# A transformer block on one core: GpSimd makes the attention factors by a power of -1, and ScalarE does some of its work at other places of a step

## The chip, the cores and the metric

The kernel runs on one core of one Trainium2 chip. The metric is the time of one execution on the device in microseconds. Before the change the median of three runs is 760.0 us (758.47 to 761.76). All times below are microseconds unless marked ns.

A core has five engines that run side by side, each in the order of its own program: TensorE (PE; its weight loads are PEld), VectorE (DVE), ScalarE (ACT), GpSimd (POOL) and SyncE (SP, which here only issues DMAs). They wait for each other by semaphores. GpSimd and ScalarE issue DMAs too.

## The reference

One block of an adaptive transformer, with x of 2048 rows and D = 640, in fp32:

```python
sa, ca, ga, sb, cb, gb = split(silu(c) @ w_mod, 6)
h = layernorm(x) * (1 + ca) + sa
x = x + ga * attention(h)
h = layernorm(x) * (1 + cb) + sb
x = x + gb * ((relu(h @ w1 + b1) ** 2) @ w2 + b2)          # F = 1728
```

Attention has 32 heads of 20 and is linear in the number of rows:

```python
q, k, v = split(h @ wqkv)                     # per head
pq, pk = q @ w_phi, k @ w_phi
phi_q = concat(softmax(pq), softmax(-pq))     # 40 features per head
phi_k = concat(softmax(pk), softmax(-pk))
kv, z = phi_k.T @ v, sum over rows of phi_k
o = (phi_q @ kv) / (phi_q @ z + 1e-6)
attention = o @ wo
```

## The kernel before

Matrix products run in fp32r with both operands split into a high and a low part: the high part is a rounding copy on ScalarE, the low part a subtraction on VectorE, and each product is made of three (high by high, high by low, low by high). So every tensor that TensorE reads goes through both engines first.

The rows are 16 tiles of 128, `t` = 0 to 15; two tiles make a step `j` = 0 to 7. The program has three parts. The first projects q, k and v of all tiles and sums `kv` and `z`. For 12 tiles the exponentials of q (`e`: two halves, of pq and of -pq, not yet normalized) go to DRAM and come back later as `el`; those of the last four tiles (`eq12` to `eq15`) stay on the chip, and the last three of them are still raw products when the second part starts. The second part, which the change edits, is the attention output. The third is the MLP of all steps.

In the second part, for each tile:

- `e_prod` (L875): VectorE multiplies `el` with a row of z (`scr`, L879) and sums within heads (`dn`, L881). GpSimd makes the common denominator `dd` of both softmaxes from these sums and the sums `rs_q` of the exponentials: two instructions for the 1e-6 term (L884, L885), then per half one product (L887) and one addition (L888).
- `e_recip` (L890): VectorE takes the reciprocal of `dd` (L894) and multiplies it with the other half's `rs_q` to the two factors `dn` (L896).
- `e_scale`: VectorE scales `e` by the factors: the last two heads to `ut` (`e_tail`, L906), the other thirty to `ezb` (`e_main`, L917). Here these scaled exponentials are called e'.

Then for each step: TensorE turns `ut` (`tail_turn`, L933), ScalarE copies the result to `ept` (L934), and TensorE multiplies that with a small part of kv (`tail_num`, L939), which ScalarE puts into the last four columns of `ezb` (L942). TensorE turns `ezb` in five groups (`te`, L951), ScalarE copies each (`ept`, L952), TensorE multiplies them with kv to `numa`, `numb`, `numc` (`num`), ScalarE copies the high half of the attention output `ot` (L974), and VectorE makes the low half (`num_lo`, L89; in steps 0 and 1 it goes another way, by TensorE and ScalarE). Last comes the product with `wo` (`do_wo`, `pwo`), which ScalarE copies to `at` (L1011) and stores.

All engines but SP follow the order in which the code of this part is written (`manual_schedule`). The loop over `j` interleaves two steps: `do_wo` of step j is cut into pieces, and at fixed places between them (`turns`) stand the tail and the `te` of step j + 1. Between those the loop places other work: `q_chain` and `exps` of the raw tiles 13 to 15 (VectorE's maximum, minimum and subtraction, ScalarE's two exponentials; `SPREAD` and `SUMS` say in which step), `p_hi` (ScalarE's high half of a weight of the MLP, L1043), `ln0` (the pieces of the first LayerNorm of the MLP: two sums, two squares, copies of the statistics, four scalings, four scalings), and `plus_x` (DMAs on GpSimd's queue that add x to the stored rows).

Of the kernel before, what the change touches and what calls it, by code (L numbers as in the profile page):

```python
# [8 lines left out]
F32 = mybir.dt.float32  # L9
# [3 lines left out]
ALU = mybir.AluOpType  # L13
AX = mybir.AxisListType

P = 128
S = 2048
D = 640
H = 32
DH = 20  # L20
F = 1728
NT = S // P
# [13 lines left out]
KEPT = NT - POSTPONED  # L36
W2_AT = 48
PLAIN = 2
DEALT = range(NT // 2)
DIRECT = 2  # L40
LAST = 3
W_AT = (
    *range(21),
# [9 lines left out]
def kernel(  # L53
# [19 lines left out]
    nc = tc.nc  # L73
# [23 lines left out]
    const = ctx.enter_context(tc.tile_pool(name="const", bufs=1))  # L97
# [10 lines left out]
    def tok2(tag, name, at=0, pool=None):  # L108

        bufs = 1  # L110
        if tag == "w":
            tag = f"w{next(w_at)}"
        elif pool is None:
            bufs = BUFS.get(tag, 1)
        t = (pool or mem).tile([P, 2 * D + (W2_AT if tag == 'late' else 128 if tag in W_LONG else 0)], F32, tag=tag, name=name, bufs=bufs)
        return t[:, at : at + 2 * D].rearrange("p (s d) -> p s d", s=2)
# [16 lines left out]
    def small(shape, tag, name, bufs=2):  # L133
        return (pc if tag in ("mx", "sk", "dn", "dd") else tiny).tile(shape, F32, tag=tag, name=name, bufs=bufs)
# [94 lines left out]
    def flat(e):  # L229
        return e.rearrange("p s d -> p (s d)")  # L230
# [27 lines left out]

    cs = const.tile([P, NC], F32, name="cs")
    ce = const.tile([P, NC], F32, name="ce")  # L260
    const.tile([P, 8], F32, name="fill")
    nc.scalar.activation(ce, c_t, AF.Exp, scale=-1.0)
    nc.vector.tensor_scalar(ce, ce, 1.0, None, op0=ALU.add)
    nc.vector.reciprocal(ce, ce)
# [114 lines left out]
    HT, PK, EK, EQ, PQ = {}, {}, {}, {}, {}  # L379
# [54 lines left out]
    def spread(t, e, nm):  # L434
        mx = small([P, 2, H], "mx", f"mx{nm}")
        nc.vector.tensor_reduce(mx[:, 0], heads(t), axis=AX.X, op=ALU.max)
        nc.vector.tensor_reduce(mx[:, 1], heads(t), axis=AX.X, op=ALU.min)
        for s in (1, 0):
            nc.vector.tensor_tensor(heads(e[:, s]), heads(t), over(mx[:, s]), op=ALU.subtract)

    def exps(e):
        nc.scalar.activation(e[:, 0], e[:, 0], AF.Exp)  # L442
        nc.scalar.activation(e[:, 1], e[:, 1], AF.Exp, scale=-1.0)
# [28 lines left out]
    def q_chain(t, whole=True):  # L472
        if t < KEPT:
            EQ[t] = tok2(f"q{t % 2}", f"eq{t}")
        e = EQ[t]
        spread(PQ[t], e, f"q{t}")
        if whole:
            exps(e)
            q_sums(t)

    def q_sums(t):
        e = EQ[t]
        s = rs_q[:, t]
        nc.vector.tensor_reduce(s, heads(flat(e)), axis=AX.X, op=ALU.add)
        if t < KEPT:
            nc.sync.dma_start(ESP[t], flat(e))
# [225 lines left out]
    for t in range(2, NT - 2):  # L712
        j, i = divmod(t, 2)
# [161 lines left out]
    def e_prod(t):  # L875
        if t >= NT:
            return
        z = SCR[t % 2]
        nc.vector.tensor_tensor(z, flat(ET[t]), flat(zb), op=ALU.mult)  # L879
        dn = DN[t] = small([P, 2, H], "dn", f"dn{t}", 3)  # L880
        nc.vector.tensor_reduce(dn.rearrange("p s h -> p (s h)"), heads(z), axis=AX.X, op=ALU.add)  # L881
        rs = rs_q[:, t].rearrange("p (s h) -> p s h", s=2)
        dd = DD[t] = small([P, H], "dd", f"dd{t}")
        nc.gpsimd.tensor_tensor(dd, rs[:, 0], rs[:, 1], op=ALU.mult)  # L884
        nc.gpsimd.tensor_scalar(dd, dd, 1e-6, None, op0=ALU.mult)  # L885
        for s in range(2):
            nc.gpsimd.tensor_tensor(dn[:, s], dn[:, s], rs[:, 1 - s], op=ALU.mult)  # L887
            nc.gpsimd.tensor_tensor(dd, dd, dn[:, s], op=ALU.add)  # L888

    def e_recip(t):  # L890
        if t >= NT:
            return
        rs = rs_q[:, t].rearrange("p (s h) -> p s h", s=2)
        nc.vector.reciprocal(DD[t], DD[t])  # L894
        for s in range(2):
            nc.vector.tensor_tensor(DN[t][:, s], rs[:, 1 - s], DD[t], op=ALU.mult)  # L896
# [26 lines left out]
    def e_scale(t):  # L923
        e_tail(t)
        e_main(t)
# [46 lines left out]
    def num_hi(j):  # L972
        for src, hi, _ in num_parts(j):
            nc.scalar.activation(hi, src, AF.Copy)  # L974

    def num_lo(j):

        if j >= DIRECT:
            for src, hi, low in num_parts(j):
# [9 lines left out]
    def do_wo(j, i, h, *hooks, a=0, b=15):  # L989
        for at, hook in hooks:  # L990
            if at > a:
                wo_part(j, i, h, a, at)
            hook()
            a = at
        if a < b:
            wo_part(j, i, h, a, b)
# [73 lines left out]
    def p_hi(n=1):  # L1070
        for _ in range(n):
            if todo["hi"]:
                prep_hi(*todo["hi"].pop(0))
# [139 lines left out]
    SPREAD, SUMS = {1: 1, 3: 2}, {3: 1, 4: 2}  # L1213
    ln0 = None
    for j in range(NB):
        nxt = j + 1 < NB
        b, c = 2 * j + 5, 2 * j + 6
        turns = {1: ((0, 0, 11), (0, 0, 15), (0, 1, 4), (0, 1, 15)), 6: ((0, 1, 2), (0, 1, 8), (0, 1, 15), (1, 0, 15)),
                 0: ((0, 1, 4), (0, 1, 10), (1, 0, 3), (1, 0, 15))}.get(j, ((0, 0, 6), (0, 0, 11), (0, 0, 15), (0, 1, 15)))
        todo_ = (lambda: tail_turn(j + 1), lambda: tail_num(j + 1), lambda: tr_e(j + 1, range(3)), lambda: tr_e(j + 1, (3, 4)))  # L1220

        def hooks(i, h):
            return [(at, f) for (i_, h_, at), f in zip(turns, todo_) if nxt and (i, h) == (i_, h_)]
        if j == 4:
            load_x1(0)
            load_dealt(0)
        if j < 5:
            p_load()
        if j != 5:
            e_prod(b)  # L1230
        e_recip(b - 1)
        e_scale(b - 1)
        if j == 6:
            mod_sum(5, gate_b)
        if j == 5:
            q_chain(KEPT + 3, False)
        load_e(b + 2)
        do_wo(j, 0, 0, *hooks(0, 0))
        if j == 5:
            exps(EQ[KEPT + 3])  # L1240
            q_sums(KEPT + 3)
            e_prod(b)
        do_wo(j, 0, 1, *hooks(0, 1))
        if j == 7:
            t2(0, 0)
            t2(0, 1)
        if j == 4:
            ln0 = ln_dealt(0)
            next(ln0)
            next(ln0)  # L1250
        if j == 6:
            next(ln0)
            turn(0, 0)
            turn(0, 1)
        if j == 2:
            exps(EQ[KEPT + 1])
        if j in SUMS:
            q_sums(KEPT + SUMS[j])
        e_prod(c)
        if j != 5:  # L1260
            e_recip(b)
            e_scale(b)
        do_wo(j, 1, 0, *hooks(1, 0))
        if j == 7:
            t2(0, 2)
            t2(0, 3)
        if nxt:
            num(j + 1)
            num_hi(j + 1)
        do_wo(j, 1, 1, b=8)  # L1270
        if j == 7:
            t2(0, 4)
            p = tp("gbt")[:NC, :P]
            nc.tensor.transpose(p, gate_b, ident)
            nc.scalar.activation(gate_r, p, AF.Copy)
            nc.sync.dma_start(GD[1], gate_r)
            nc.sync.dma_start(gb_b, GD[1].rearrange("c p -> (c p)")[None, :].to_broadcast([P, D]))
        if not nxt:
            do_wo(j, 1, 1, a=8)
        if nxt:  # L1280
            do_wo(j, 1, 1, a=8, b=11)
            num_lo(j + 1)
            do_wo(j, 1, 1, a=11)
        if j == 5:
            e_recip(b)
            e_scale(b)
        if 1 <= j < 6:
            p_hi()
        if j in SPREAD:
            q_chain(KEPT + SPREAD[j], False)  # L1290
            if j > 1:
                exps(EQ[KEPT + SPREAD[j]])
        load_e(c + 2)
        if j:
            plus_x(j - 1)
        if j == 4:
            next(ln0)
            next(ln0)
            next(ln0)
        if j == 5:  # L1300
            next(ln0)
        if j == 5:
            p_lo(4)
            p_load(4)
        if j == 6:
            p_hi(4)
            p_lo(5)
            p_load(3)
        if j == 7:
            p_load(2)  # L1310
# [42 lines left out]
    def plain(j, n):  # L1353
        return j < PLAIN or n == NF // 2 - 1 or j == NB - 1 and n >= NF // 2 - LAST

# [133 lines left out]
    def down_pair(j, n, part):  # L1489
        v, w = W2[2 * n], W2[2 * n + 1]  # L1490
        last = n == (NF // 2 - 2 if j < NB - 1 else NF // 2 - 1 - LAST)
        if part:
# [138 lines left out]
    for j in range(NB):  # L1631
# [5 lines left out]
        for n in range(NP):  # L1637
# [53 lines left out]
            if j == NB - 1 and n == 1:  # L1691
                for k in range(NP - LAST, NP - 1):
                    plain_load(k)
            if j == NB - 1 and n == 3:
                for k in range(NP - LAST, NP - 1):
                    plain_split(k)
# [33 lines left out]
            if m == NP - 1:  # L1730
                for i in range(2):
                    add_bias(j - 1, i)
            if j == NB - 1 and n == NP - LAST:
                first_combos(j)
# [61 lines left out]
```

## Time and profile before

| what | before |
|---|---|
| median of three runs | 760.0 us |
| the profiled execution, its own time | 760.65 us |
| its span, from first to last instruction | 758.9 us |
| mean granted clock of TensorE | 0.995 |
| busy: PE / DVE / ACT / POOL | 99% / 80% / 60% / 22% |

The page of the profile gives busy time per engine. TensorE's matmuls are pipelined and their ends modelled, so "busy" includes short waits between them. A timeline row is: start, duration, engine, line, operation, output<-input, shape, count, and in brackets the idle time of the engine before it with what ended that. A row of waits is: who waited for whom, microseconds in total, times, longest. The granted clock is the share of full speed that TensorE's clock was given.

### The profile page before, as it was taken

The page shows a single profiled execution, that of the slowest core. Times are in us where ns is not written, and L with a number is a line of the kernel's source. Part 1 is how long each engine was busy: PE and PEld are TensorE (multiplying, and loading weights), DVE is VectorE, ACT ScalarE, POOL GpSimd, SP SyncE. Part 2 cuts the span into 40 slices and gives each one's busy share as a digit, 9 for nine tenths or more (in the row PEclk, how much of TensorE's full clock was granted, in tenths as well). Part 3 has the DMA queues.
Part 4 walks back from the last instruction along what each step waited for, and adds up shares of the span by engine and source line. Part 5 has one row for each costly group of instructions (what it writes and reads, how often), then busy time and mean ns, then how long its engine had stood idle before and what let it go on. Part 6 is the DMA issues. An engine that isn't in the chain of part 4 may idle for free.

```text
span 758.9 us, 15323 instructions
## 1 busy us (share of the span) xinstructions
PE 749.2 (99%) x5854; PEld 731.0 (96%) x5854; DVE 604.2 (80%) x1115; ACT 458.7 (60%) x1065; POOL 165.4 (22%) x361
## 2 busy tenths in 40 slices
PE   9999999999999999989999999999999999999998
PEld 9999999999999988878899999999999999999997
DVE  6598997988999899996756768787777777777766
ACT  5767666677852365546677757576474756647431
POOL 3000101000100347534303030132221313213110
PEclk9999999999999999999999999999999999999999
DMA  8812431343432254744777376897677777667460
GB/s 329 328 49 83 148 104 54 105 140 106 138 105 71 88 173 159 164 112 105 191 187 231 112 207 230 273 308 201 191 211 202 214 200 209 185 182 215 129 188 35
DMA packets 58796, 126.39 MB, mean 167 GB/s; under 512 B 7438, under 2 KB 16403, under 8 KB 58723
## 3 DMA queue, kind: packets, MB, share of 16 engines
q1 hardware_dynamic: 38636, 79.20, 31.8%
q0 software_dynamic: 17504, 40.90, 21.6%
q10 hardware_dynamic: 2583, 5.30, 1.9%
q8 instruction: 46, 0.75, 0.4%
q14 instruction: 27, 0.22, 0.1%
HBM read 100.74 MB, written 29.89 MB: 172 GB/s over the span
## 4 chain that ended last, share of the span: by engine, by line
PE 84%; DVE 10%; ACT 2%; POOL 2%; issue 1%; DMA 1%; ACTq 0%; POOLq 0%
PE up L79 23%; PE acc L79 17%; PE pk L79 9%; PE pv L79 9%; PE pq L79 8%; PE acc3x L79 5%; PE pwo L79 3%; PE kvp L456 3%; DVE dn L881 2%; DVE scr L879 2%; DVE ezb L917 2%; PE te L951 1%; PE foldk L281 1%; DMA ring_b<-td_b 1%; PE ta L363 1%
## 5 line engine op out<-in xcount | busy, mean ns | idle before, releaser
L79 PE MATMUL up<-h,w 128*128 128x256 f32 x1640 | 204.6, 277 | 0.1
L79 PEld LDWEIGHTS up<-h,w 128*128 128x128 f32 x1640 | 196.5, 188 | 0.7 <-DVE h L89 0.5
L1345 ACT ACTIVATE ft<-up,b_t 128x256 f32<-128x256 f32 x104 | 48.9, 471 | 96.6 <-PE up L79 96.1
L79 PE MATMUL acc<-w,ra 128*128 128x384 f32 x452 | 97.5, 335 | 0.0
L79 PE MATMUL pwo<-wo,ot 128*128 128x384 f32 (+1 forms) x480 | 79.9, 318 | 0.3 <-DVE ot L89 0.3
L1346 DVE TENSOR_TENSOR ft<-ft 128x256 f32<-128x256 f32 x104 | 44.1, 424 | 43.2 <-ACT ft L1345 41.7
L79 PE MATMUL pq<-wq,hT 128*128 128x384 f32 (+1 forms) x480 | 75.6, 312 | 0.0
L79 PEld LDWEIGHTS pwo<-wo,ot 128*128 128x128 f32 x480 | 70.9, 193 | 3.5 <-issue 2.7
L79 PEld LDWEIGHTS acc<-w,ra 128*128 128x128 f32 x452 | 72.7, 188 | 0.9 <-DVE ra L89 0.6
L79 PE MATMUL pk<-wk,hT 128*128 128x384 f32 (+1 forms) x480 | 72.7, 308 | 0.0
L79 PEld LDWEIGHTS pq<-wq,hT 128*128 128x128 f32 x480 | 71.1, 188 | 0.6 <-issue 0.2
L79 PE MATMUL pv<-wv,hT 128*128 128x384 f32 (+1 forms) x480 | 71.6, 307 | 0.0
L79 PEld LDWEIGHTS pk<-wk,hT 128*128 128x128 f32 x480 | 70.5, 188 | 0.4 <-issue 0.2
L79 PEld LDWEIGHTS pv<-wv,hT 128*128 128x128 f32 x480 | 70.0, 188 | 0.0
L89 DVE TENSOR_TENSOR ra<-ft,ra 128x384 fp32r<-128x384 f32 (+2 forms) x86 | 36.8, 448 | 32.7 <-ACT ra L1369 19.4
L1455 POOL DMA_DIRECT2D ring_a<-td_a x34 | 18.5, 543 | 117.3 <-PE acc L79 103.6
L1369 ACT ACTIVATE ra<-ft 128x384 fp32r<-128x384 f32 x48 | 25.2, 525 | 28.4 <-DVE ft L1346 22.4
L79 PE MATMUL acc3x<-w,ra 128*128 128x256 f32 x231 | 39.5, 278 | 0.0
L79 PEld LDWEIGHTS acc3x<-w,ra 128*128 128x128 f32 x231 | 37.2, 188 | 0.0
L1360 DVE TENSOR_TENSOR ft<-ft 128x128 f32<-128x128 f32 x136 | 33.3, 286 | 1.2
L447 DVE TENSOR_REDUCE sk<-ek 128x64 f32<-128x1280 f32 x16 | 23.8, 1484 | 12.8 <-ACT ek L442 10.8
L340 POOL TENSOR_SCALAR sma<-sma 128x2 f32<-128x2 f32 x6 | 1.7, 284 | 137.3 <-ACT xb L339 137.3
(269 smaller groups left out, 1474.5 us busy)
## 6 DMA issues: line engine op xcount, KB each, us to landing
ring_c<-td_c POOLq DMA_DIRECT2D x34, 384.0 KB, 3.9
ring_a<-td_a POOLq DMA_DIRECT2D x34, 384.0 KB, 3.4
ring_b<-td_b POOLq DMA_DIRECT2D x34, 256.0 KB, 3.6
esp<-eq SPq DMA_DIRECT2D x12, 640.0 KB
el<-esp SPq DMA_DIRECT2D x12, 640.0 KB
rw<-in_w SPq DMA_DIRECT2D x23, 320.0 KB
wm<-in_w_mod SPq DMA_DIRECT2D x20, 320.0 KB
xb<-in_x SPq DMA_DIRECT2D x8, 640.0 KB
```

The source lines that it names most:

```text
L79: nc.tensor.matmul(o, a, b, start=first and i == 0, stop=last and i == len(terms) - 1, skip_group_check=skip,)
L89: (eng or nc.vector).tensor_tensor(out_lo, full, hi.bitcast(F32), op=ALU.subtract)
L447: nc.vector.tensor_reduce(s, heads(flat(e)), axis=AX.X, op=ALU.add)
L456: nc.tensor.matmul(kvp[g // 4][64 * c : 64 * c + 64, a : a + 2 * n].rearrange("p (s n) -> p s n", s=2), v[:, u], e[:, :, o : o + n], start ...
L879: nc.vector.tensor_tensor(z, flat(ET[t]), flat(zb), op=ALU.mult)
L881: nc.vector.tensor_reduce(dn.rearrange("p s h -> p (s h)"), heads(z), axis=AX.X, op=ALU.add)
L917: nc.vector.tensor_tensor(EU[t][:, :, :120].rearrange("p u (s h d) -> p s u h d", s=2, d=DH), ET[t][:, :, :600].rearrange("p s (u h d) -> ...
L1345: nc.scalar.activation(r, p, AF.Relu, bias=b1_t[:, f : f + 1])
L1346: nc.vector.tensor_tensor(r, r, r, op=ALU.mult)
L1360: nc.vector.tensor_tensor(t[:, o], t[:, a], t[:, b], op=op)
L1369: nc.scalar.activation(a[:, 0, :3], t[:, :3], AF.Copy)
L1455: nc.gpsimd.dma_start(RING[j, n, r], TD[n][r].bitcast(F32R))
```

## The change

It has two parts. The first: for tiles 2 to 15 GpSimd no longer hands `dd` to VectorE. It raises `dd` to the power -1 (a column of -1.0 in an existing small tile, filled once at the start) and makes the two factors itself; `e_recip` does nothing for these tiles. The second moves work in the loop:

```diff
@@ const
-    const.tile([P, 8], F32, name="fill")
+    fill = const.tile([P, 8], F32, name="fill")
+    mone = fill[:, :1]
+    nc.gpsimd.memset(mone, -1.0)
@@ e_prod
             nc.gpsimd.tensor_tensor(dd, dd, dn[:, s], op=ALU.add)
+        if t >= POWERS:
+            nc.gpsimd.tensor_tensor(dd, dd, mone.to_broadcast([P, H]), op=ALU.pow)
+            for s in range(2):
+                nc.gpsimd.tensor_tensor(dn[:, s], rs[:, 1 - s], dd, op=ALU.mult)
@@ e_recip
-        if t >= NT:
+        if t >= NT or t >= POWERS:
             return
@@ the loop over j, from its start
         do_wo(j, 0, 0, *hooks(0, 0))
+        if j - 1 in SPREAD:
+            exps(EQ[KEPT + SPREAD[j - 1]])
...
-        if j == 2:
-            exps(EQ[KEPT + 1])
+        if 1 <= j < 6 and j != 4:
+            p_hi()
+        if j == 5:
+            next(ln0)
...
             e_scale(b)
+        if j in SPREAD:
+            q_chain(KEPT + SPREAD[j], False)
         do_wo(j, 1, 0, *hooks(1, 0))
...
             num_hi(j + 1)
+        if j == 4:
+            next(ln0)
+            next(ln0)
+            next(ln0)
+        if j == 5:
+            p_hi()
         do_wo(j, 1, 1, b=8)
...
-        if 1 <= j < 6:
-            p_hi()
-        if j in SPREAD:
-            q_chain(KEPT + SPREAD[j], False)
-            if j > 1:
-                exps(EQ[KEPT + SPREAD[j]])
         load_e(c + 2)
         if j:
             plus_x(j - 1)
-        if j == 4:
-            next(ln0)
-            next(ln0)
-            next(ln0)
-        if j == 5:
-            next(ln0)
```

POWERS is 2. The order of TensorE and of SP is the same before and after. Three places show how the order of the others moves. In the rows, the number behind `dd`, `dn`, `el`, `eq`, `at` is that of the tile, behind `ut`, `ot`, `ept`, `te` that of the step (a second number is the group), and what follows the underscore is the buffer.

GpSimd at tile 2, between its denominator and the start of tile 3; before:

```order
L887 TENSOR_TENSOR dn2_3254<-dn2_3254,rs_q_106 128x32
L888 TENSOR_TENSOR dd2_3256<-dd2_3256,dn2_3254 128x32
L887 TENSOR_TENSOR dn2_3254<-dn2_3254,rs_q_106 128x32
L888 TENSOR_TENSOR dd2_3256<-dd2_3256,dn2_3254 128x32
L884 TENSOR_TENSOR dd3_3369<-rs_q_106 128x32
L885 TENSOR_SCALAR dd3_3369<-dd3_3369 128x32
L887 TENSOR_TENSOR dn3_3367<-dn3_3367,rs_q_106 128x32
```

and after:

```order
L890 TENSOR_TENSOR dn2_3255<-dn2_3255,rs_q_106 128x32
L891 TENSOR_TENSOR dd2_3257<-dd2_3257,dn2_3255 128x32
L890 TENSOR_TENSOR dn2_3255<-dn2_3255,rs_q_106 128x32
L891 TENSOR_TENSOR dd2_3257<-dd2_3257,dn2_3255 128x32
L893 TENSOR_TENSOR dd2_3257<-dd2_3257,fill_180 128x32
L895 TENSOR_TENSOR dn2_3255<-rs_q_106,dd2_3257 128x32 x2
L887 TENSOR_TENSOR dd3_3373<-rs_q_106 128x32
L888 TENSOR_SCALAR dd3_3373<-dd3_3373 128x32
```

Behind the sum in `dd2` now come the power (with `fill`, which holds -1.0) and the two factors, and tile 3 starts behind these.

VectorE at the end of step 1, from the factors of tile 7 to the chain of tile 13; before:

```order
L894 RECIPROCAL dd7_3584<-dd7_3584 128x32
L896 TENSOR_TENSOR dn7_3582<-rs_q_106,dd7_3584 128x32 x2
L906 TENSOR_TENSOR ut3_3594<-el7_3420,dn7_3582 128x80
L917 TENSOR_TENSOR ezb3_3155<-el7_3420,dn7_3582 128x2x10x60
L89 TENSOR_TENSOR ot2_3713<-numa2_3714,ot2_3713 128x2x256
L89 TENSOR_TENSOR ot2_3713<-numb2_3715,ot2_3713 128x2x256
L89 TENSOR_TENSOR ot2_3713<-numc2_3716,ot2_3713 128x256
L436 TENSOR_REDUCE mxq13_3751<-eq13_2828 128x32
L437 TENSOR_REDUCE mxq13_3751<-eq13_2828 128x32
L439 TENSOR_TENSOR eq13_2828<-eq13_2828,mxq13_3751 128x640 x2
```

and after:

```order
L913 TENSOR_TENSOR ut3_3598<-el7_3424,dn7_3586 128x80
L924 TENSOR_TENSOR ezb3_3156<-el7_3424,dn7_3586 128x2x10x60
L439 TENSOR_REDUCE mxq13_3699<-eq13_2829 128x32
L440 TENSOR_REDUCE mxq13_3699<-eq13_2829 128x32
L442 TENSOR_TENSOR eq13_2829<-eq13_2829,mxq13_3699 128x640 x2
L90 TENSOR_TENSOR ot2_3723<-numa2_3724,ot2_3723 128x2x256
L90 TENSOR_TENSOR ot2_3723<-numb2_3725,ot2_3723 128x2x256
L90 TENSOR_TENSOR ot2_3723<-numc2_3726,ot2_3723 128x256
```

The reciprocal and the two products of tile 7 are gone, and the chain of tile 13 (`mxq13`, `eq13`) stands ahead of the low halves of `ot2`.

ScalarE from the end of step 3 into step 4, where `w1_2` is the high half of an MLP weight, `eq14` the exponentials of tile 14 and `ept5_5` the copy of the turned tail; before:

```order
L952 ACTIVATE ept4_3_4023<-te4_3_4022 124x512
L952 ACTIVATE ept4_4_4030<-te4_4_4029 124x512
L1011 ACTIVATE at7_4054<-pwo7_0_4052 128x384
L974 ACTIVATE ot4_4071<-numa4_4072 128x2x256
L974 ACTIVATE ot4_4071<-numb4_4073 128x2x256
L974 ACTIVATE ot4_4071<-numc4_4074 128x256
L1011 ACTIVATE at7_4054<-pwo7_1_4053 128x256
L1013 DMA a1_7_211<-at7_4054 128x640
L1043 ACTIVATE w1_2_3760<-rw1_2_3761 128x640
L442 ACTIVATE eq14_2829<-eq14_2829 128x640
L443 ACTIVATE eq14_2829<-eq14_2829 128x640
L934 ACTIVATE ept5_5_4158<-tail5_4157 80x256
```

and after:

```order
L959 ACTIVATE ept4_3_4027<-te4_3_4026 124x512
L959 ACTIVATE ept4_4_4034<-te4_4_4033 124x512
L1050 ACTIVATE w1_2_3764<-rw1_2_3765 128x640
L1018 ACTIVATE at7_4064<-pwo7_0_4062 128x384
L981 ACTIVATE ot4_4081<-numa4_4082 128x2x256
L981 ACTIVATE ot4_4081<-numb4_4083 128x2x256
L981 ACTIVATE ot4_4081<-numc4_4084 128x256
L1018 ACTIVATE at7_4064<-pwo7_1_4063 128x256
L1020 DMA a1_7_212<-at7_4064 128x640
L941 ACTIVATE ept5_5_4160<-tail5_4159 80x256
```

with the exponentials a little further on, in step 4:

```order
L959 ACTIVATE ept5_1_4186<-te5_1_4185 124x512
L959 ACTIVATE ept5_2_4193<-te5_2_4192 124x512
L445 ACTIVATE eq14_2830<-eq14_2830 128x640
L446 ACTIVATE eq14_2830<-eq14_2830 128x640
L1018 ACTIVATE at8_4152<-pwo8_1_4151 128x256
```

The weight's half has moved ahead of `at7`, and the exponentials behind the third `ept5` of the turned groups; between the high halves of `ot4` and the tail's copy `ept5_5` stand only the second half of `at7` and its store.

More of the change, by code (lines that the diff above doesn't have):

```diff
@@ L40 @@
 DIRECT = 2
+POWERS = 2
 LAST = 3
```

## The prediction

> **What bounds the kernel now.** I read the page's shares first, then the stages, then what TensorE waits for, then the timelines of the attention steps.
>
> ```profile
> span 758.9 us, 15323 instructions
> ...
> PE 749.2 (99%) x5854; PEld 731.0 (96%) x5854; DVE 604.2 (80%) x1115; ACT 458.7 (60%) x1065; POOL 165.4 (22%) x361
> ...
> PE 84%; DVE 10%; ACT 2%; POOL 2%; issue 1%; DMA 1%; ACTq 0%; POOLq 0%
> ```
>
> TensorE is busy for 749.2 of 758.9 us. The profiled execution took 760.65 us, so 1.75 us lie around the span; it stands 0.65 above the median of 760.0, and I take that off at the end.
>
> The windows (wall time, then busy time of PE, PEld, DVE, ACT, POOL, then granted clock) show which stretch has anything to give:
>
> ```profile
> 338.00:341.00 3.00, 3.00 (x16) 3.00 (x15) 3.00 (x3) 1.53 (x3) 1.32 (x2) 0.50 0.04 9
> ...
> 250.00:392.00 142.00, 137.30 (x992) 123.53 (x988) 121.19 (x172) 81.03 (x187) 62.44 (x128) 0.98 0.55 146
> 392.00:758.00 366.00, 362.98 (x2838) 361.51 (x2838) 268.80 (x646) 215.69 (x513) 77.89 (x165) 1.00 0.68 197
> ```
>
> From 392 us on the change edits nothing, and TensorE idles for 3 of 366 us. In the attention stretch, 250 to 392, it idles for 142.0 - 137.3 = 4.7 us, and there are microseconds with the granted clock at 0.50. The waits of TensorE from 270 to 392 (us in total, times, longest) are these:
>
> ```profile
> PE tail L939 <- ACT ept L934: 4.4, 3, 2.8
> PE pwo L79 <- DVE ot L89: 0.3, 1, 0.3
> ```
>
> So three waits are for ScalarE's copy of the turned tail (`ept`, L934) and one is for VectorE's low half of the attention output (`ot`, L89): 4.4 + 0.3 = 4.7 us, all the idle time there is. The timeline of TensorE has their places:
>
> ```profile
> 276.26 0.38 PE L933 MATMUL tail<-ident,ut 128*80 128x128 f32 x2
> ...
> 300.21 3.02 PE L79 MATMUL pwo<-wo,ot 128*128 128x256 f32 x21
> ...
> 314.26 2.33 PE L79 MATMUL pwo<-wo,ot 128*128 128x256 f32 x17
> ...
> 318.91 0.54 PE L939 MATMUL tail<-kvd,ept 80*128 80x40 f32 x4
> ...
> 326.66 1.08 PE L79 MATMUL numa<-ept,kvd 124*64 124x256 f32 x8
> ...
> 335.85 0.64 PE L939 MATMUL tail<-kvd,ept 80*128 80x40 f32 x4 [2.76 <-ACT ept L934]
> ...
> 345.35 1.08 PE L79 MATMUL numa<-ept,kvd 124*64 124x256 f32 x8
> ...
> 353.30 0.64 PE L939 MATMUL tail<-kvd,ept 80*128 80x40 f32 x4 [1.52 <-ACT ept L934]
> ...
> 362.86 1.08 PE L79 MATMUL numa<-ept,kvd 124*64 124x256 f32 x8
> ```
>
> From the tail product (L939) to the first `numa` of the same step is the same work in each step. It takes 326.66 - 318.91 = 7.75 us in the step without a wait, 345.35 - 335.85 = 9.50 after the wait of 2.76, and 362.86 - 353.30 = 9.56 after that of 1.52. The extra 1.75 + 1.81 = 3.6 us is the halved clock, which comes some 2 us after each gap. The two gaps with their aftermath, and the two small waits, cost 4.7 + 3.6 = 8.3 us. That is all that the ScalarE part can bring.
>
> The Trainium skill (TensorE: Matmul & The Clock Gate, Part 1: The HAM clock gate) says that the clock is halved after an idle window of about 3.4 us. By that rule neither gap would have halved it, and closing them would bring 4.7 us. This trace disagrees: 0.50 after gaps of 2.76 and 1.52 us.
>
> **ScalarE's part.** The timeline of ScalarE has what stands ahead of the late tail copies (335.44 and 352.89):
>
> ```profile
> 324.06 1.09 ACT L952 ACTIVATE ept<-te 124x512 f32<-124x512 f32 x2 [0.40 <-PE te L951]
> ...
> 331.78 0.74 ACT L1043 ACTIVATE w<-rw 128x640 fp32r<-128x640 f32 x1 [0.40 <-ACT at L1011]
> 334.17 0.74 ACT L442 ACTIVATE eq<-eq 128x640 f32<-128x640 f32 x1 [1.65 <-DVE eq L439]
> ...
> 335.44 0.36 ACT L934 ACTIVATE ept<-tail 80x256 f32<-80x256 f32 x1
> ...
> 350.48 0.74 ACT L1043 ACTIVATE w<-rawt 128x640 fp32r<-128x640 f32 x1 [0.40 <-ACT at L1011]
> 351.12 0.81 ACT L1152 ACTIVATE junk<-xm,smb 128x640 f32<-128x640 f32 x1
> ...
> 352.89 0.36 ACT L934 ACTIVATE ept<-tail 80x256 f32<-80x256 f32 x1
> ```
>
> At 331.78 come a weight's high half (0.74) and the exponentials of eq14, of which the first waits 1.65 us for VectorE's subtraction; then the tail copy, wanted at about 332.2. The change puts the weight half ahead of `at7`'s first half and the exponentials behind the third `ept` of the next step. Nothing is left ahead of the tail copy, so the 2.76 and its 1.75 go. At 350.48 the weight half (0.74) and two squares (351.12 to 352.9) are moved likewise: the squares ahead of `at9`'s second half, the weight half one step on. `at9` ends at about 350.6 instead of 350.1, the tail copy can start at about 351, and its product was due at 351.8: the 1.52 and its 1.81 go.
>
> What the new places cost: two exponentials (pitch 0.64, some 1.4 us together) stand ahead of the last two `ept`, which ended at 324.06 + 1.09 = 325.15 for a `numa` at 326.66. That is 1.5 us of cover; TensorE's own products hide them, with 0.1 to spare, and without cover they cost up to 1.4 in each of two steps. The weight halves and the four LayerNorm scalings fall into ScalarE's waits for TensorE. The stores that ScalarE issues behind them go out up to 1.4 us later, and their readers (the residual adds on GpSimd) come a step later. SP's order is unchanged.
>
> **VectorE's part.** One tile's work is these rows, and then the chain of q for tile 13 (302.56 to 305.72, 3.16 us):
>
> ```profile
> 281.72 1.49 DVE L881 TENSOR_REDUCE dn<-scr 128x64 f32<-128x1280 f32 x1
> 283.12 0.34 DVE L894 RECIPROCAL dd<-dd 128x32 f32<-128x32 f32 x1
> 283.50 0.29 DVE L896 TENSOR_TENSOR dn<-rs_q,dd 128x32 f32<-128x32 f32 x2
> 283.82 0.24 DVE L906 TENSOR_TENSOR ut<-el,dn 128x80 f32<-128x80 f32 x1
> 283.98 1.46 DVE L917 TENSOR_TENSOR ezb<-el,dn 128x1200 f32<-128x1200 f32 x1
> 285.36 1.54 DVE L879 TENSOR_TENSOR scr<-el,zb 128x1280 f32<-128x1280 f32 x1
> ...
> 302.56 0.80 DVE L436 TENSOR_REDUCE mxq<-eq 128x32 f32<-128x640 f32 x1
> ...
> 305.72 1.48 DVE L879 TENSOR_TENSOR scr<-el,zb 128x1280 f32<-128x1280 f32 x1
> ...
> 367.13 0.24 DVE L906 TENSOR_TENSOR ut<-eq,dn 128x80 f32<-128x80 f32 x1
> ```
>
> Removed from each of 14 tiles are the reciprocal and two products: 283.82 - 283.20 = 0.62 us, 8.7 in all. Left per tile is `ut` + `ezb` 1.6, `scr` 1.45, reduction 1.5: 4.6 us. The chain of q for tiles 13 and 14 comes ahead of the low halves of `ot`, no longer behind. From step 2 on VectorE has room for it: two tiles and the low halves are about 2 x 4.6 + 1.5 = 10.7 us against 14.05 of TensorE's step (the runs at 300.21 and 314.26 stand at one place of two steps).
>
> **GpSimd's part, which sets the early steps.** Each of these tiles gets a power and two products on GpSimd. What a GpSimd instruction costs depends on what VectorE does beside it:
>
> ```profile
> 271.67 0.25 POOL L888 TENSOR_TENSOR dd<-dd,dn 128x32 f32<-128x32 f32 x1
> ...
> 273.46 0.25 POOL L888 TENSOR_TENSOR dd<-dd,dn 128x32 f32<-128x32 f32 x1
> ...
> 283.87 0.31 POOL L887 TENSOR_TENSOR dn<-dn,rs_q 128x32 f32<-128x32 f32 x1
> 284.25 1.30 POOL L888 TENSOR_TENSOR dd<-dd,dn 128x32 f32<-128x32 f32 x1
> 285.51 1.50 POOL L884 TENSOR_TENSOR dd<-rs_q 128x32 f32<-128x32 f32 x1
> ```
>
> An instruction of 0.25 us takes 1.30 where `ezb` runs on VectorE and 1.50 where `scr` does; each time it ends 0.1 us behind VectorE's instruction. So while VectorE runs `ut`, `ezb`, `scr`, one GpSimd instruction gets through at each border. The power itself is in the trace with 2 columns only:
>
> ```profile
> L346 POOL TENSOR_TENSOR sqa<-sqa,mhalf x6: 707/709/1353, 61.7 to 195.9; 128x2 f32<-128x2 f32 x6
> ...
> L1156 POOL TENSOR_TENSOR rn<-smb,rn x8: 194/196/273, 355.0 to 684.8; 128x2 f32<-128x2 f32 x8
> ```
>
> Call its price with 32 columns P. A product takes 0.19 with 2 columns and 0.25 with 32, so the lowest P is 0.71 + 0.06 = 0.77, if what the power adds (0.51) is there once. The highest is 0.19 + 32 x 0.256 = 8.4, if the 0.51 is paid per column. I take 0.77, by the row it is nearest to: the only power row, widened as the product is. Both ends are carried on, the high one as a rival.
>
> Tile 2: its sum is done at 271.92, so its factors come at 271.92 + 0.07 + P + 0.55 = 272.6 + P. Tile 3 then needs GpSimd's six instructions (271.92 to 273.71 before: 1.8 us, 0.3 each). One of the first three is held until `ut` and `ezb` of tile 2 are through, 1.7 us on; three or four more take 0.9 to 1.2, then P and 0.6: 3.2 to 3.5 + P, so 276.0 + 2P, where `ut` of tile 3 started at 275.81 before. TensorE's tail turn stood at 276.26 and now waits for about 276.3 + 2P = 277.8.
>
> Tile 4: `ezb`, `scr`, reduction, `scr`, reduction (7.5 us) give its denominators and those of tile 5, and GpSimd's last instructions, one held by the `scr`, end 7.65 + P behind tile 3's. Tiles 5, 6 and 7: between factors stand `ut` and `ezb` (1.7 with one instruction held), `scr` (1.4, another), then three short ones (0.9), P and 0.55, so 4.7 + P each, in place of 4.6 + 0.62 = 5.2. Tile 7 has its factors at 276.0 + 2P + 7.65 + P + 3 x (4.7 + P) = 297.75 + 6P. Then `ut` and `ezb` (1.6), the chain of q (3.16), and the first low half of `ot` (0.7): 303.2 + 6P. TensorE asked for it 2.33 us behind the start of the run at 300.21, as in the step where it had to wait (the run of 17 from 314.26): 302.5. It comes 0.7 + 6P = 5.3 us late at P = 0.77. The wait at the tail turn lies within this.
>
> That is two new gaps, of about 1.5 us and over. Each should halve the clock as the old ones did, for some 1.75 us. The first loss is made up while VectorE is the later one anyway; the second counts: +1.7. After that VectorE is ahead and the chain of q for tile 14 is hidden.
>
> **The sum.** -4.7 - 3.6 + 5.3 + 1.7 = -1.3 us: 759.4 against the profiled 760.65, 758.7 against the median. By the Trainium skill's rule for the clock it would be -4.7 + 5.3 = +0.6. I forecast **759 us, no change that can be told** (0.5%, 3.8 us, is about what a measurement here can tell). For P up to 1.6 the sum stays under +3.8.
>
> **The rivals.**
> *Faster: the factors are in time.* If VectorE reaches the low half of step 2 early enough, because GpSimd's instructions are held less often than I count or its queue runs ahead, only the 8.3 goes: 760 - 8.3 = 752, or 754 with a short wait left. For it: VectorE has 0.62 us less to do per tile, 3.7 by tile 7, and the chain of q takes only 3.16. Against it: the rows of 1.30 and 1.50 above.
> *Slower: the power's price grows with its columns.* The place is tiles 3 to 7; each us of P costs 6 us there. It decides from P = 1.6. At P = 2.5 it is 0.7 + 15 + 1.7 - 8.3 = +9.1, so 769. At 8.4 every tile would take 4.7 + 8.4 = 13.1 us on GpSimd against 7.0 on TensorE; twelve tiles behind tile 3 at 293 bring the last to about 450 where its `ut` was at 367 (the last row of VectorE's), and the kernel to about 840. For it: 0.51 us more for two columns. Against it: nothing tells one-off from per-column cost.
> *The gaps stay.* The exponentials delay the last `ept` by more than their cover, so that `numa` waits in two steps and the clock halves again: the 8.3 is not won, and with 5.3 + 1.7 the time is about 767.
>
> **How the numbers follow.** Forecast 0.36, faster rival 0.34, slower rival 0.25, gaps stay 0.05. Faster: 0.33 of the rival and 0.03 of the forecast's low edge, 0.36. Same: 0.31 of the forecast and 0.01 of the faster rival, 0.32. Slower: 0.25 + 0.05 + 0.02 = 0.32. The range goes from all 8.3 won, 751, to P about 2.8, 771; dearer powers, about 0.1, are left out. The forecast alone holds 757 to 764.
>
> **What would show it.** Right: no wait on L934's copy at the old places; granted clock 1.0 around 338 and 355; a power row of 0.7 to 1.0 us; TensorE idle for 1 to 2 us before tile 3's tail turn and again at the first low half of step 2, on GpSimd and VectorE. Wrong: a power row over 1.6 us, VectorE waiting for GpSimd in every step, or no early gap at all.

## The result and the profile after

The changed kernel takes 809.07 us (median of four runs, 808.02 to 809.77) where the kernel before took 759.24 beside it (four runs, 757.29 to 761.76). The ratio is 1.0648, 95% interval 1.0628 to 1.0669: **slower by 6.5%**, where the forecast was no change, 759 us in 751 to 771.

The page of the changed kernel, with the shares of the chain that ended last and the group of the new power:

```profile
span 807.9 us, 15328 instructions
...
PE 758.1 (94%) x5854; PEld 738.3 (91%) x5854; DVE 596.0 (74%) x1073; ACT 458.1 (57%) x1065; POOL 249.9 (31%) x404
...
PE 77%; POOL 16%; DVE 4%; issue 1%; ACT 1%; DMA 1%; SPq 0%; ACTq 0%; POOLq 0%
...
L893 POOL TENSOR_TENSOR dd<-dd,fill 128x32 f32<-128x32 f32 x14 | 77.6, 5541 | 1.1
```

GpSimd's share of the chain was 2% and is 16% now. The last row has the reason: 14 powers take 5541 ns each in the mean (13 of them 5.43 to 5.46 us, one 6.80). The prediction had taken 770 ns.

The windows (wall time, busy time of PE, PEld, DVE, ACT, POOL, then granted clock) say where the time lies:

```profile
250.00:441.00 191.00, 146.50 (x993) 131.44 (x989) 112.94 (x129) 80.14 (x186) 146.89 (x171) 0.87 0.41 109
441.00:807.00 366.00, 363.07 (x2839) 361.39 (x2838) 268.89 (x646) 215.92 (x513) 77.84 (x165) 1.00 0.68 197
```

The MLP takes 366 us as before. All of the loss is in the attention stretch: 191.0 us in place of 142.0, so +49.0. Of these, TensorE's idle time is 191.0 - 146.5 = 44.5 in place of 4.7 (+39.8), and its busy time 146.5 in place of 137.3 (+9.2): the same matmuls at a lower granted clock (0.87 in place of 0.98, means over the stretch with its idle time).

What TensorE waited for, and then VectorE between 260 and 441 us (total, times, longest):

```profile
PE pwo L80 <- DVE ot L90: 20.6, 3, 10.1
PE tail L940 <- DVE ut L913: 20.6, 4, 8.5
PE numb L80 <- ACT ept L959: 3.3, 1, 3.3
```

```profile
DVE ut L913 <- POOL dn L895: 62.6, 12, 7.4
```

The three waits of TensorE are 44.5 us, all of its idle time. None is the wait for ScalarE's tail copy any more. TensorE waits for VectorE, and VectorE waits for GpSimd's factors at 12 of 14 tiles. The timelines of VectorE and TensorE have the places:

```profile
278.15 0.27 DVE L913 TENSOR_TENSOR ut<-el,dn 128x80 f32<-128x80 f32 x1 [5.56 <-POOL dn L895]
287.17 0.27 DVE L913 TENSOR_TENSOR ut<-el,dn 128x80 f32<-128x80 f32 x1 [7.43 <-POOL dn L895]
300.18 0.28 DVE L913 TENSOR_TENSOR ut<-el,dn 128x80 f32<-128x80 f32 x1 [5.56 <-POOL dn L895]
...
330.42 0.27 DVE L913 TENSOR_TENSOR ut<-el,dn 128x80 f32<-128x80 f32 x1 [5.55 <-POOL dn L895]
...
333.50 1.72 DVE L442 TENSOR_TENSOR eq<-eq,mxq 128x640 f32<-128x640 f32 x2
335.14 0.68 DVE L90 TENSOR_TENSOR ot<-numa,ot 128x512 fp32r<-128x512 f32 x1
...
399.58 0.24 DVE L913 TENSOR_TENSOR ut<-eq,dn 128x80 f32<-128x80 f32 x1 [5.93 <-POOL dn L895]
...
417.45 0.24 DVE L913 TENSOR_TENSOR ut<-eq,dn 128x80 f32<-128x80 f32 x1 [5.21 <-POOL dn L895]
```

```profile
287.50 0.43 PE L940 MATMUL tail<-ident,ut 128*80 128x128 f32 x1 [8.53 <-DVE ut L913]
...
335.88 1.65 PE L80 MATMUL pwo<-wo,ot 128*128 128x384 f32 x4 [10.11 <-DVE ot L90]
...
407.03 1.08 PE L80 MATMUL numb<-ept,kvd 124*64 124x256 f32 x8 [3.28 <-ACT ept L959]
```

One tile of GpSimd in the middle of it:

```profile
314.32 5.44 POOL L893 TENSOR_TENSOR dd<-dd,fill 128x32 f32<-128x32 f32 x1
319.84 0.47 POOL L895 TENSOR_TENSOR dn<-rs_q,dd 128x32 f32<-128x32 f32 x2
320.26 0.26 POOL L887 TENSOR_TENSOR dd<-rs_q 128x32 f32<-128x32 f32 x1
320.61 1.48 POOL L888 TENSOR_SCALAR dd<-dd 128x32 f32<-128x32 f32 x1
322.17 1.29 POOL L890 TENSOR_TENSOR dn<-dn,rs_q 128x32 f32<-128x32 f32 x1
...
324.41 5.43 POOL L893 TENSOR_TENSOR dd<-dd,fill 128x32 f32<-128x32 f32 x1
```

The power takes 5.44 us by itself. From one power to the next are 324.41 - 314.32 = 10.09 us, of which 4.65 are not the power: two instructions held by VectorE's `ezb` and `scr` (1.48 and 1.29) and short ones. TensorE needs 7.0 us per tile (14.05 us per step of two tiles in the profile before), so GpSimd now sets the pace.

### The profile page after: what moved, and what is told of

Its sections match the earlier page's. It is cut to its first block, busy times and chain, and to the rows that moved or that the text cites. A ratio compares the mean times of both kernels' runs of the same rounds, so it can differ in the third digit from the quotient of the medians.

```text
span 807.9 us, 15328 instructions
## 1 busy us (share of the span) xinstructions
PE 758.1 (94%) x5854; PEld 738.3 (91%) x5854; DVE 596.0 (74%) x1073; ACT 458.1 (57%) x1065; POOL 249.9 (31%) x404
## 4 chain that ended last, share of the span: by engine, by line
PE 77%; POOL 16%; DVE 4%; issue 1%; ACT 1%; DMA 1%; SPq 0%; ACTq 0%; POOLq 0%
PE up L80 23%; PE acc L80 17%; POOL dd L893 10%; PE pk L80 9%; PE pv L80 9%; PE pq L80 7%; PE acc3x L80 5%; PE kvp L459 2%; POOL dn L890 2%; POOL dd L888 2%; PE pwo L80 1%; POOL dd L891 1%; PE ta L366 1%; POOL dn L895 1%; DVE dn L884 1%
## 5 line engine op out<-in xcount | busy, mean ns | idle before, releaser
L80 PE MATMUL pwo<-wo,ot 128*128 128x384 f32 (+1 forms) x480 | 87.4, 336 | 20.6 <-DVE ot L90 20.6
L80 PEld LDWEIGHTS pwo<-wo,ot 128*128 128x128 f32 x480 | 76.4, 206 | 24.7 <-DVE ot L90 21.6
L893 POOL TENSOR_TENSOR dd<-dd,fill 128x32 f32<-128x32 f32 x14 | 77.6, 5541 | 1.1
L913 DVE TENSOR_TENSOR ut<-el,dn 128x80 f32<-128x80 f32 x12 | 3.1, 262 | 50.9 <-POOL dn L895 50.9
```

What stands on the lines that cost most here:

```text
L80: nc.tensor.matmul(o, a, b, start=first and i == 0, stop=last and i == len(terms) - 1, skip_group_check=skip,)
L893: nc.gpsimd.tensor_tensor(dd, dd, mone.to_broadcast([P, H]), op=ALU.pow)
```

## The experiments

The theory (A): the power costs about 0.39 us + 0.158 us per column (0.71 for the two columns shown before, 5.44 for 32), and this price alone makes the loss. The moves in the loop gain a little, and that GpSimd makes the factors costs nothing by itself. The rivals: that the hand-over to GpSimd or its port conflicts with VectorE make the loss whatever the operation is (B), or that the moved work does (C). Each ratio below is against executions of the kernel before that were taken together with the run.

**The moves alone.** The changed kernel without its first part:

```diff
-POWERS = 2
+POWERS = NT
```

> Only the second part of the change: POWERS is set to the number of tiles, so VectorE makes all factors by the reciprocal as before, while the weight parts, the exponentials, the LayerNorm pieces and the chain of q stand at their new places. Theory A (the power's price is the whole loss, and the two late gaps are closed by the moves): 8.3 us of the gaps go; the chain of q for tile 13 now stands ahead of the low half of step 2, which comes 301.0 + 3.2 + 0.6 = 304.8 where TensorE asks at 302.5, so 2.3 us of waiting and 1.7 of halved clock come in: -4.3, about 755. Theory C (the moves on ScalarE do harm of their own, or the gaps stay): 760 or more, with a wait of TensorE for the tail's copy still in the profile.

Measured: 756.34 us (754.91 to 756.79, eight runs), ratio 0.9962 (0.9947 to 0.9976). The moves are no loss; C falls. TensorE's timeline has two gaps left between 250 and 442 us:

```profile
304.79 0.97 PE L80 MATMUL pwo<-wo,ot 128*128 128x384 f32 x4 [2.46 <-DVE ot L90]
...
335.39 0.97 PE L80 MATMUL pwo<-wo,ot 128*128 128x384 f32 x4 [0.40 <-DVE ot L90]
```

VectorE's timeline there has the subtractions of that chain and the low half behind them:

```profile
302.38 1.76 DVE L442 TENSOR_TENSOR eq<-eq,mxq 128x640 f32<-128x640 f32 x2
304.05 0.68 DVE L90 TENSOR_TENSOR ot<-numa,ot 128x512 fp32r<-128x512 f32 x1
```

And the windows behind the first gap:

```profile
306.00:308.00 2.00, 2.00 (x12) 2.00 (x10) 1.97 (x2) 0.38 (x1) 0.00 (x0) 0.60 1.02 244
308.00:310.00 2.00, 2.00 (x9) 1.90 (x9) 1.93 (x6) 0.72 (x3) 1.18 (x4) 0.54 0.60 124
```

The clock is close to half (0.60 and 0.54) behind the gap of 2.46. Both waits for the tail copy are gone, as predicted. In their place the chain of q for tile 13, which now stands ahead of the low half of `ot`, opens a gap of 2.46 us in step 2.

**The power alone.** The kernel before with only the first part of the change, its loop as it was.

```diff
+        if t >= POWERS:
+            nc.gpsimd.tensor_tensor(dd, dd, mone.to_broadcast([P, H]), op=ALU.pow)
+            for s in range(2):
+                nc.gpsimd.tensor_tensor(dn[:, s], rs[:, 1 - s], dd, op=ALU.mult)
```

> Only the first part of the change: the power and the two products on GpSimd from tile 2 on, with the loop as before. Theory A: GpSimd's chain sets the pace from tile 2 to tile 15, so the order of the loop hardly matters: the factors of tile 7 at 330 as in the changed kernel, 806 to 809 us. Theory C (a large part of the loss comes from the moves, which put the chain of q ahead of the low halves): 795 or less.

Measured: 811.05 us (810.15 to 811.12), ratio 1.0681 (1.0659 to 1.0703). The whole loss is in this part; the time is 2 us above the 806 to 809 that were expected. TensorE waits for the same tensors of VectorE as in the changed kernel, and twice for the tail copy, a wait that the moves take away:

```profile
PE tail L940 <- DVE ut L913: 21.0, 4, 8.7
PE pwo L80 <- DVE ot L90: 15.4, 3, 7.9
PE tail L946 <- ACT ept L941: 3.6, 2, 2.1
```

**Another operation in the power's place.** The changed kernel with a product where the power stood; its factors are then not those of the reference, and everything else is the same work.

```diff
-            nc.gpsimd.tensor_tensor(dd, dd, mone.to_broadcast([P, H]), op=ALU.pow)
+            nc.gpsimd.tensor_tensor(dd, dd, mone.to_broadcast([P, H]), op=ALU.mult)
```

> The changed kernel with a product in place of the power (dd times -1, so the factors are not those of the reference): the same instructions at the same places, the same crossings between the engines, and 0.25 us instead of 5.44. Theory A: the sum of the prediction with P = 0.25 is 0.7 + 1.5 = 2.2 us late at step 2, 1.7 of clock if that gap halves it, 8.3 gone: -4.4, so 755, or 753 if the clock stays. Theory B (handing the factors to GpSimd costs by itself, by its held instructions and two more crossings per tile): 765 or more.

Measured: 753.87 us (753.12 to 754.39), ratio 0.9929 (0.9913 to 0.9946). The group of the operation, and the larger of TensorE's two gaps:

```profile
L893 POOL TENSOR_TENSOR dd<-dd,fill 128x32 f32<-128x32 f32 x14 | 3.4, 241 | 1.1
```

```profile
304.19 0.96 PE L80 MATMUL pwo<-wo,ot 128*128 128x384 f32 x4 [1.42 <-DVE ot L90]
```

At 241 ns in place of 5541, with the same hand-overs and order, and with GpSimd's instructions held as before (1.48 and 1.29 to 1.30 us in this profile too), 55 us are gone. B falls: it is the duration of this one operation.

**Half the columns.** The power on the first 16 of the 32 columns; the other 16 heads keep their denominator where a factor should stand.

```diff
-            nc.gpsimd.tensor_tensor(dd, dd, mone.to_broadcast([P, H]), op=ALU.pow)
+            nc.gpsimd.tensor_tensor(dd[:, : H // 2], dd[:, : H // 2], mone.to_broadcast([P, H // 2]), op=ALU.pow)
```

> The changed kernel with the power over the first 16 of the 32 columns (the other 16 heads keep the denominator itself, so their factors are not those of the reference). Theory A, price by the column: from 0.71 for 2 and 5.44 for 32 columns 0.39 + 0.158 each, so 2.9 for 16; the sum gives 0.7 + 6 x 2.9 = 18.1 late at step 2, 1.7 of clock, 8.3 gone: +11.5, so 771, and up to 4 more in the later steps (7.6 us per tile against 7.0): 771 to 776. Theory B, a price per instruction that does not depend on the columns (5.4 for this exponent or for a broadcast one): 808.

Measured: 775.93 us (775.36 to 778.29), ratio 1.0218 (1.0194 to 1.0243). GpSimd's rows of one tile and the next:

```profile
303.99 2.92 POOL L893 TENSOR_TENSOR dd<-dd,fill 128x16 f32<-128x16 f32 x1
...
311.55 2.91 POOL L893 TENSOR_TENSOR dd<-dd,fill 128x16 f32<-128x16 f32 x1
```

The price of 16 columns is the one that the line through 2 and 32 gives, 0.39 + 16 x 0.158 = 2.92. A tile takes 311.55 - 303.99 = 7.56 us, again 4.64 + P. The time is at the upper end of the 771 to 776 that go with this price, and far from the 808 of a price per instruction.

**The price by itself.** The kernel before with powers whose results nothing reads, put where GpSimd idles; lines 266, 633 to 635 and 669 to 671 of this kernel.

```diff
+    nc.gpsimd.tensor_tensor(spare, ones[:, :32], mone.to_broadcast([P, 32]), op=ALU.pow)
...
+    nc.gpsimd.tensor_tensor(spare[:, :16], ones[:, :16], mone.to_broadcast([P, 16]), op=ALU.pow)
+    nc.gpsimd.tensor_tensor(spare[:, :8], ones[:, :8], mone.to_broadcast([P, 8]), op=ALU.pow)
+    nc.gpsimd.tensor_tensor(spare, ones[:, :32], mhalf[:, :1].to_broadcast([P, 32]), op=ALU.pow)
...
+            nc.gpsimd.tensor_tensor(spare, ones[:, :32], fill2[:, :32], op=ALU.pow)
+            nc.gpsimd.tensor_tensor(spare, ones[:, :32], mone.to_broadcast([P, 32]), op=ALU.mult)
+            nc.gpsimd.tensor_tensor(spare[:32], ones[:32, :32], mone[:32].to_broadcast([32, 32]), op=ALU.pow)
```

> The kernel before, with seven extra GpSimd instructions whose results nothing reads, put where GpSimd idles (0 to 60 us): powers of a tile of ones, and one product. Theory A, the power's price is 0.39 us + 0.158 us for each column, whatever the exponent is, however it is read and whatever the data: 128x32 with the exponent -1 read as one repeated column 5.44 us; 128x16 2.92; 128x8 1.65; 128x32 with the exponent -0.5 5.44; 128x32 with the exponent a full tile of -1 5.44; the product of 128x32 0.25; 32 partitions x 32 columns with the exponent -1 5.44, since columns count and not elements. Rival D, the price hangs on the repeated column or on the exponent: then the full tile, or the exponent -0.5, differs from 5.44 by over 0.5 us. Rival E, the price goes with the number of elements: 32 partitions then take under 2 us.

The kernel was executed once (761.76 us); what counts here are its rows. GpSimd's timeline:

```profile
7.73 5.45 POOL L266 TENSOR_TENSOR fill<-ones,fill 128x32 f32<-128x32 f32 x1
...
15.37 2.90 POOL L633 TENSOR_TENSOR fill<-ones,fill 128x16 f32<-128x16 f32 x1
18.35 1.63 POOL L634 TENSOR_TENSOR fill<-ones,fill 128x8 f32<-128x8 f32 x1
20.06 5.41 POOL L635 TENSOR_TENSOR fill<-ones,mhalf 128x32 f32<-128x32 f32 x1
...
30.72 5.45 POOL L669 TENSOR_TENSOR fill<-ones,fill 128x32 f32<-128x32 f32 x1
36.24 0.92 POOL L670 TENSOR_TENSOR fill<-ones,fill 128x32 f32<-128x32 f32 x1
37.23 5.87 POOL L671 TENSOR_TENSOR fill<-ones,fill 32x32 f32<-32x32 f32 x1
```

Neither the exponent, nor how it is read, nor the data change the price (D falls), and a quarter of the partitions is no cheaper (E falls): it goes by columns. Two rows are longer than expected: the product took 0.92 in place of 0.25, and the 32 partitions 5.87 in place of 5.44. Two-input subtractions of VectorE ran where both began, as with the instructions of 1.30 and 1.50 in the profile before; for these two rows that cause is argued and not shown (the last section has a power that was held so).

**The power from tile 8 on.**

```diff
-POWERS = 2
+POWERS = 8
```

> The changed kernel with the power from tile 8 on only; tiles 2 to 7 keep VectorE's reciprocal. Theory A, each tile that has the power costs GpSimd's chain of about 11 us, against 8.3 us for a tile without it (seven tiles from tile 8 on: 77.9 us in the changed kernel's profile, 57.8 in the kernel before's), so that 7 x 2.9 = 20 us come on top of the 756.3 us of the loop without the power, and some 2 us of halved clock: 778 us, range 774 to 782. Rival F, only the first steps suffer, where the tiles have no lead, and later ones have slack for it: 756 to 760 us.

Measured: 778.36 us (777.26 to 778.48), ratio 1.0243 (1.0221 to 1.0265). F falls: with the early steps spared, the later eight tiles still cost 1.0243 - 0.9962 = 0.028 of the time, some 21 us, over the moves alone. There is no slack in them either, since GpSimd's chain of some 10 us per tile stands against TensorE's 7.

**The moves without the new gap.** The moves alone, with q's chain of step 1 back at its old place; that of step 3 stays ahead.

```diff
-        if j in SPREAD:
+        if j == 3:
             q_chain(KEPT + SPREAD[j], False)
         do_wo(j, 1, 0, *hooks(1, 0))
...
+        if j == 1:
+            q_chain(KEPT + SPREAD[j], False)
         load_e(c + 2)
```

> The changed kernel without the power, and with q's chain of step 1 (two VectorE instructions) back at its old place at the end of the step; q's chain of step 3 stays ahead. Theory A, the one gap of 2.5 us that the loop without the power had left (TensorE waiting for the low half of ot in step 2 behind that chain) goes, with the 1 us of halved clock after it: 756.3 - 3.5 = 752.8 us, range 751.5 to 754.5; no gap of TensorE over 1 us between 250 and 380 us. Rival G, the low half is late for another reason, or the exponentials of step 2 then come late for q's sums: 756 us or more.

Measured: 755.34 us (753.81 to 757.10), ratio 0.9942 (0.9921 to 0.9964). This is a miss: 751.5 to 754.5 was expected, and no gap over 1 us. The gap of step 2 is gone, but the one of step 4, which had been 0.40, has grown to 1.91, and the clock is halved behind it:

```profile
333.20 1.65 PE L80 MATMUL pwo<-wo,ot 128*128 128x384 f32 x4 [1.91 <-DVE ot L90]
```

```profile
334.00:336.00 2.00, 2.00 (x8) 1.84 (x8) 1.97 (x3) 0.38 (x1) 0.00 (x0) 0.50 1.07 199
```

With both chains ahead, TensorE's wait in step 2 had given VectorE time: between 276 and 336 us VectorE waited 2.1 us for ScalarE's high halves of `ot`. In this profile it waits for nothing in that stretch, so its own work sets the low halves, and the chain of 3 us still ahead of them costs in step 4.

**Only ScalarE's moves.** Both chains of q back at their old place.

```diff
-        if j in SPREAD:
-            q_chain(KEPT + SPREAD[j], False)
         do_wo(j, 1, 0, *hooks(1, 0))
...
+        if j in SPREAD:
+            q_chain(KEPT + SPREAD[j], False)
         load_e(c + 2)
```

> The same with q's chains of steps 1 and 3 both at their old place, so that of the change only the moves on ScalarE are left. Theory A: the last gap of 0.4 us at step 4 goes too: 752.4 us, range 751 to 754.5. Rival G: a chain of q that comes later makes the exponentials, which stand ahead of the next step's second half, hold ScalarE's queue, and the time is 755 us or more.

Measured: 753.75 us (752.71 to 755.31) against 759.8, ratio 0.9923 (0.9904 to 0.9942): 0.8% faster than the kernel before, and the lowest median here of a kernel that computes the reference. One gap is left in TensorE's timeline between 250 and 395 us, in step 5, and the clock stays at 1.00 behind it:

```profile
346.00 0.96 PE L80 MATMUL pwo<-wo,ot 128*128 128x384 f32 x4 [1.19 <-DVE ot L90]
```

```profile
346.00:348.00 2.00, 2.00 (x11) 1.71 (x12) 1.93 (x7) 0.38 (x1) 1.68 (x7) 1.00 0.53 210
348.00:350.00 2.00, 2.00 (x18) 1.97 (x17) 2.00 (x3) 0.91 (x4) 1.81 (x5) 1.00 0.03 8
```

The time is in A's range of 751 to 754.5, and the gap of step 4 is gone, but A had no gap of 1.19 in step 5. TensorE has no wait for ScalarE in that stretch, so the exponentials in the next step held nothing up: G falls.

## Why the prediction was wrong

**The step that failed** is "I take 0.77, by the row it is nearest to". The power of 32 columns takes 5.44 us. The prediction had the bounds 0.77 and 8.4 and put the 0.51 us that a power of two columns costs over a product down as one-off. Between 2 and 32 columns it is 4.73 us for 30, so 0.158 us for each column, and 0.39 once. The low bound needed one special case, all of the surplus one-off; any share of it per column is paid for every column. A ninth of the way to the high bound, 0.77 + 7.63 / 9 = 1.6, was enough for the rival to decide. All sixteen powers in the profile before (lines 346, 562 and 1155) have two columns, so it had no second width to tell; the value belonged between the ends, and the rival at 0.25 had too small a chance. The range also left out powers above 2.8.

**The formulas around P were right**, each within 0.3 us up to step 2. With 5.44 in them, and the measured start behind: factors of tile 2 at 272.6 + P = 278.0 (`ut` 278.15); tile 3 at 276.0 + 2P = 286.9 (287.17); tile 4 another 7.65 + P = 13.1 later (13.0); tile 7 at 297.75 + 6P = 330.4 (330.42); the first low half of step 2 done at 303.2 + 6P = 335.8 and so begun at 335.1 (335.14). The rest of the loss is the slower rival's: 4.7 + P = 10.1 us per tile on GpSimd against 7.0 on TensorE. Its count of twelve tiles behind tile 3 gives 286.9 + 13.1 + 11 x 10.1 = 411 for tile 15; it came at 417.45, where it stood at 367.13 before. That is +50.3, about the +49.0 of the stretch; the 6 us beyond the count are not followed up here.

**Point by point.**
- *What bounds the kernel*: right. The loss is in the stretch 250 to 392 alone, and the MLP did not move.
- *ScalarE's part*: right in its mechanism. The waits at the tail copy are gone wherever these moves are made. Its size was 8.3 us; the kernel with only these moves gained 0.58% to 0.96%, or 4.4 to 7.3 us. A new wait of 1.19 us for VectorE's low half took some of it. The 3.6 us of halved clock in the 8.3 were read from one execution, and not every execution of the kernel before lost them (see the last point).
- *The cover of the exponentials*, 1.5 us for 1.4: right. No `numa` or `numb` of steps 2 and 4, where the exponentials of tiles 13 and 14 now stand, waits in the changed kernel or in the one with ScalarE's moves only. The changed kernel's wait of 3.28 us at 407.03 is another one: ahead of those copies stand the exponentials of tile 15, at the same place as before the change. VectorE made the subtraction for them at 402.63, behind a `ut` (399.58) that had waited 5.93 us for GpSimd.
- *VectorE's part*: the chain of q ahead of the low half was said to hide after step 2. With VectorE's own reciprocals it does not: 2.46 in step 2 with 0.40 in step 4, or 1.91 in step 4 where step 2 is spared. The 0.62 us per tile would have helped: with a cheap operation in the power's place the gap of 2.46 is 1.42, and the time 753.87.
- *GpSimd's part*: the holds by VectorE were right (4.65 us per tile beside the power, predicted 4.7), the price of the power wrong.
- *The halved clock*: right in kind, wrong in amount. It was to cost 1.7 us where the profile before had 3.6; with gaps of 2 to 10 us TensorE's busy time in the stretch is 9.2 us longer than before. The Trainium skill (TensorE: Matmul & The Clock Gate, Part 1: The HAM clock gate) asks for an idle window of about 3.4 us. These runs show 0.50 to 0.60 after gaps of 1.91 and 2.46 too, so it did not take that long here; after 1.19 and 1.42 they show 1.00. (The prediction's sum by that rule had no halving at all, though its second gap, 5.3 - 1.5 = 3.8 us, was longer than the window.) One thing the prediction took as fixed: the mean granted clock differs between executions of one kernel. Of the 24 executions of the kernel before that stand beside the experiments, four have 0.999 or 1.000 and take 757.07 to 757.43 us; the others have 0.994 to 0.998 and take 758.09 to 761.52. So a gap of 1.5 to 2.8 us seems not to halve the clock every time; no trace of such an execution of that kernel is kept to show it.

## What to carry to other kernels

An operation that the profile shows in one small shape only has an unknown slope: when its count on the path is 6 or 14, carry the slope's bounds into the forecast and not the price of the small shape. A narrow operation between two engines that hand on to TensorE is worth moving only if the receiving engine's whole chain per tile, holds included, stays under TensorE's time per tile (here 4.65 + P against 7.0, so P under 2.4); the first steps, which had no lead here and pay 6P, can ask for less (1.6 by the prediction's sum). And a change of two parts should be tried by parts: here one of them gained 0.4%, and the other lost 6.8%.

## What the hardware did that was not expected

- GpSimd's power costs by the column: 0.71 us for 2, 1.63 for 8, 2.90 to 2.92 for 16 and 5.41 to 5.46 for 32 columns of 128 partitions, where a product of 32 takes 0.24. With 32 partitions it is no cheaper (5.87). By the Trainium skill (GPSIMD Engine Reference, 1. Specifications) each of its cores owns 16 partitions, and a price that does not fall with the partitions agrees with that.
- A power that is under way does not hold VectorE's two-input instructions here. While one ran on GpSimd, from 333.44 to 338.88, VectorE's two subtractions took 1.72 us (row 333.50 above); where no power ran, in the kernel with the moves alone, they took 1.76 (row 302.38). But a power that starts together with such an instruction is held itself: the one beside `scr` below took 6.80 us, 1.36 over 5.44, and VectorE its usual 1.47. The kernel with the power alone has the same pair (6.79), and so has the one with 16 columns (4.28 in place of 2.92).

```profile
333.44 5.44 POOL L893 TENSOR_TENSOR dd<-dd,fill 128x32 f32<-128x32 f32 x1
...
353.42 6.80 POOL L893 TENSOR_TENSOR dd<-dd,fill 128x32 f32<-128x32 f32 x1
```

```profile
353.44 1.47 DVE L882 TENSOR_TENSOR scr<-el,zb 128x1280 f32<-128x1280 f32 x1
```

The Trainium skill (SBUF — State Buffer, SBUF: two separate sides) says that of a VectorE instruction with two inputs in SBUF and a GpSimd instruction that reads SBUF, whichever starts first has the shared ports for its whole instruction. For GpSimd's instructions that wait for VectorE the rows agree (1.48 and 1.29 in place of 0.29 and 0.25); for VectorE beside a power that started first they do not (1.72). Which of the two was first at 353.42 and 353.44, the rows do not tell.
